# Another order of slots in the first half item, and a group's turns and stores taken in the last item

## The chip, the core and the metric

The kernel runs on one core of a Trainium2 chip. The metric is the device time of one execution in microseconds, as the median of the runs. A core has TensorE (PE in the rows, its weight loads PEld), VectorE (DVE), ScalarE (ACT), GpSimd (POOL) and SyncE (SP), which here issues nearly all DMAs. Each engine works through a program of its own in order and waits on semaphores.

## The reference, cut to what matters

```python
def phi(x):                                # q, k: (4, 4, 1088, 32), r = 8
    a, b = x @ S1.T, x @ S2.T
    return outer(a, b).reshape(..., 64)
num = phi(q) @ (phi(k).T @ v)
den = phi(q) @ phi(k).sum(axis=2) + 1e-6
x = (num / den) -> (4352, 128)             # the heads side by side

P = exp(x @ w_gate - max)                  # (4352, 8 experts)
for _ in range(8):
    P /= P.sum(1) + 1e-9; P /= P.sum(0) + 1e-9; P *= 4352 / 8
out = 0
for e in range(8):
    out += P[:, e:e+1] * (maximum(x @ w1[e], 0) @ w2[e])   # 128 -> 1024 -> 128
```

The weights of expert e are (128, 1024) and (1024, 128), everything is float32. Almost all of the work is the two products of eight experts.

## The kernel before, in words

The attention, the routing and a first part of the experts' work run in the first 189 us. The rest, 189 to 880 us, is the function `weighted`, and the change lies in it alone.

**Groups, items, half items.** The tokens that are left stand in seven groups (`wgroups`), numbered 0 to 6, each with two blocks of n tokens and a list of experts. An item is one expert on one group; there are 40. An item has two half items (s = 0, 1), so t runs from 0 to 79. Group 0 has n = 320, group 4 has n = 320, group 5 has n = 224 and six items (t = 66 to 77), group 6 (`LAST`) has the same tokens as group 5, one expert, and the half items 78 and 79. Its sums are made in another way (`whole`).

**First and second products.** `firsts(t)` makes the products of one half item with the first weights: seven (item 0: eight) products into two PSUM tiles, `pair0` and `pair1`, which ScalarE and VectorE empty. L1171 is the relu on ScalarE, L1174 the sum with relu on VectorE (custom instruction), L1243 to L1252 are copies. They give h0 to h3, and VectorE makes four differences of them, t0 (L1216), t1 (L1219), t2 (L1220) and t3 (L1223). `seconds(t)` multiplies these with the second weights (L1311) and adds the products up in four PSUM tiles, `acc[g][0..3]`, called sums 0 to 3 here.

**Slots.** `seconds(t)` has seven slots. Each slot holds two products of row half 0 and two of row half 1 (rho = 0, 1: partitions 0 to 63 and 64 to 127 of h). The table `order` says which sum m each row half works on in each slot; a 3 stands once for a row half, 0, 1 and 2 twice. Sum 0 needs h0 and h2, sum 1 needs h1 and t0, sum 2 needs t1 and t2, sum 3 needs t3. In TensorE's program the slots of `seconds(t - 1)` alternate with the products of `firsts(t)`, one by one (item 0's second half item starts with two first products, and so does the next).

**The hand-over of a sum.** Both row halves add to the same sum. After the first row half is done with sum m, ScalarE copies one column of it to a tile `turn` (L1363). Nobody uses the value: the other row half's products wait for that copy, and so come after.

**Ring.** h and t live in ten places of the tile `hb`. `turns[t]` lists the seven places of half item t, in the order h0, h2, h3, t0, h1, t2, t3 (t1 replaces h3). A place that an earlier half item has used is free once that one's slots have read it.

**The output of a group.** When a group's four sums are complete, they are copied to SBUF (L1391, L1393), halves of them change places by DMA (`swap_half`, L1412), and `finish_seven` puts nine small sums on the list `leisure`, then for each of the two blocks a sum with the kept part (all L1467) and a turn: `put` turns 32x32 blocks on VectorE (L1495) and issues its stores on SP at once (L738; put off only before item 38). For group 4 the first turn gives eight stores and the second four. An entry of `leisure` whose flag is False, which the turns have, is not taken by GpSimd; it waits at the list's head until VectorE takes it. `aside` gives entries to GpSimd, once or twice in a half item. `spare`, called twice in a half item (after L1216's and after L1223's place), gives VectorE an entry.

**The end.** Group 5's sums are finished in the last item, by begin_next_to_last (L1425) and finish_next_to_last: row sums on VectorE (L1398), `swap_half` in two pairs of DMAs (L1412), the first after sums 0 and 1, the second after 2 and 3, then four sums on GpSimd (L1434), of which the third and fourth need the second pair, one more on VectorE (L1435). `begin_last` adds the results with L1511; behind it on VectorE stand the last sums of group 6 (L1505), the last turns (L1520) and their stores (L738 on SP and ACT).

Of the kernel before, what the change touches and what calls it, by code (L numbers as in the profile page):

```python
# [52 lines left out]
def kernel(  # L53
# [68 lines left out]
    own = consts.tile([P, H], F32, name="own")  # L122
# [36 lines left out]
    for i in range(2):  # L159
        t = wk.tile([P, H + 1, NT + 1, D], F32, name=f"v{i}", bufs=1)  # L160
# [482 lines left out]
    LAST = len(wgroups) - 1  # L643
# [81 lines left out]
    def one_store():  # L725
        if stores:
            stores.pop(0)()
# [348 lines left out]
    def sum_x(i, part_):  # L1076
        xf = sources[i]
        if part_ == 0:
            nc.gpsimd.tensor_tensor(xf[:, 4:6], xf[:, 1:4:2], xf[:, 0:2], op=Alu.subtract)  # L1079
        elif part_ == 1:  # L1080
            nc.vector.tensor_tensor(xf[:, 6], xf[:, 3], xf[:, 4], op=Alu.subtract)
        else:
            nc.vector.tensor_tensor(xf[:, 7], xf[:, 2], xf[:, 6], op=Alu.subtract)
# [27 lines left out]
    def weighted():  # L1111
# [5 lines left out]
        leisure, chores = [(lambda engine, do=do: do(), False) for do in left], []  # L1117
# [8 lines left out]
        for t in range(len(todo)):  # L1126
            if t:
                a0, a1, a2, a3, a4, a5, a6 = turns[-1]
                f0, f1, f2 = unused
                now = [f1, a4, f0, f2, a0, a1, a3] if t == 1 else [f0, f1, f2, a0, a1, a4, a3]  # L1130
                unused = [a2, a5, a6]
            else:
                now, unused = unused[:7], unused[7:]
            turns.append(now)
# [7 lines left out]
        def firsts(t):  # L1142

            i, s = todo[t]
            g, e = witems[i]
            n = wgroups[g][1]
# [29 lines left out]
            def leave(engine, anywhere=False):  # L1176
                if leisure and leisure[0] is None:
                    leisure.pop(0)
                elif leisure and (anywhere or leisure[0][1]):
                    leisure.pop(0)[0](engine)  # L1180
                    return True
# [27 lines left out]
            def spare(spot):  # L1209
                if s == 1 and i + 1 < len(witems):  # L1210
                    sum_x(i + 1, 1 + spot)
                if 0 < g < LAST and (leisure and leisure[0] and not leisure[0][1] if g + 1 == LAST else s == 0):
                    leave(nc.vector, True)

            def first_of_h():
# [66 lines left out]
        def seconds(t):  # L1282

            i, s = todo[t]
            g, e = witems[i]
            lo, n, es = wgroups[g]
# [3 lines left out]
            def fetch(part_):  # L1290
                if coming is not None:
                    load_second(coming, part_)
# [23 lines left out]
            if g in whole and last:  # L1316
                begin_last(g)
                for u, cols in ((0, (0, n)), (1, (0, 128)), (1, (128, n))):
                    m = u + 2 * (cols[0] > 0)
# [24 lines left out]
            def tiles(rho, m, r):  # L1344
                if m == 3:
                    for half in range(2):
                        into(rho, 3, half, raw(1, 1, half), ts[3], half)
                    return
                for half, (f, x) in enumerate((((raw, 0, 0), h[0]), ((raw, 0, 1), h[2]), ((form, 3), h[1]),
                                               ((form, 0), ts[0]), ((form, 2), ts[1]),  # L1350
                                               ((form, 1), ts[2]))[2 * m:2 * m + 2]):
                    into(rho, m, half, f[0](*f[1:], r), x, r)

            order = ((0, 0, 1, 1, 2, 2, 3),) * 2 if narrow(g) else ((0, 0, 2, 2, 1, 1, 3), (1, 1, 3, 0, 0, 2, 2))
            full = [max(k for line in order for k in range(7) if line[k] == m) for m in range(4)]
            for at in range(7):
                for rho in range(2):
                    m = order[rho ^ t % 2][at]
                    tiles(rho, m, order[rho ^ t % 2][:at].count(m))
                yield  # L1360
                if not narrow(g):
                    for m in {1: (0, 1) if t == 0 else (0,), 3: (2,)}.get(at, ()):
                        nc.scalar.copy(turn, acc[g][m][:, 0:1])  # L1363
                for m in range(4):
                    if full[m] == at:
                        fetch(m)
                        if last:
                            ended(g, m)
                for q in range(2 if last else 0):
                    if at == max(full[2 * q:2 * q + 2]) + (narrow(g) and q == 0):  # L1370
                        if narrow(g):
                            add_rows(g, q)
                        swap_half(g, q)
                if last and at == 5 and g + 1 == LAST:
                    begin_next_to_last(g)
                if last and at == 6:
                    (finish_next_to_last if g + 1 == LAST else finish_seven)(g)
                yield
# [3 lines left out]
        def narrow(g):  # L1382
            return 2 * wgroups[g][1] <= 512

        def ended(g, m):
            n = wgroups[g][1]
            if g not in ends:
                ends[g] = late[0].tile([P, 4 * NW], F32, tag="z", name="z", bufs=1)[:, 0:4 * n].rearrange(
                    "p (m n) -> p m n", m=4)
            if not narrow(g):  # L1390
                nc.scalar.copy(ends[g][:, m], acc[g][m][:, 0:n])  # L1391
            elif m % 2:
                nc.scalar.copy(ends[g][:, m - 1:m + 1].rearrange("p m n -> p (m n)"), acc[g][m // 2][:, 0:2 * n])  # L1393

        def add_rows(g, q):
            n = wgroups[g][1]
            z = ends[g][:, 2 * q:2 * q + 2].rearrange("p m n -> p (m n)")
            nc.vector.tensor_tensor(z, acc[g][2 + q][:, 0:2 * n], z, op=Alu.add)  # L1398

        def swap_half(g, q):  # L1400

            n = wgroups[g][1]
            z = ends[g].rearrange("p m n -> p (m n)")[:, 2 * n * q:2 * n * (q + 1)]
            if q == 0:
                swapped.clear()
            if q == 0 or g + 1 < LAST:
                swapped.append(wpool.tile([P, F], F32, tag="w1", name="w1"))
            w = swapped[-1]
            for to, from_, at, lo, hi in ((((lower, upper, n, 0, 2 * n), (upper, lower, 2 * n, 0, n)),
                                           ((lower, upper, 0, 0, n), (upper, lower, 0, 0, 2 * n)))[q] if g + 1 == LAST  # L1410
                                          else ((lower, upper, 0, 0, 2 * n), (upper, lower, 0, 0, 2 * n))):
                nc.sync.dma_start(out=w[to, at:at + hi - lo], in_=z[from_, lo:hi])  # L1412
# [33 lines left out]
        def finish_seven(g):  # L1446
            settle(g)
            n = wgroups[g][1]
            z = ends[g]
            held = []  # L1450

            def own(k, rows=slice(0, P)):
                if not held:
                    held.extend(room(tag, n) for tag in "zxmwf")
                return held[k][rows]

            leisure.extend([None] * 3)
            v = [z[:, m] for m in range(4)]
            x = [w[:, n * a:n * (a + 1)] for w in swapped for a in range(2)]
            lo_, up = lower, upper  # L1460

            def plus_own(k, rows, a, b, op=Alu.add):

                def of(what):
                    return own(what, rows) if isinstance(what, int) else what[rows]

                leisure.append((lambda engine: engine.tensor_tensor(own(k, rows), of(a), of(b), op=op), True))  # L1467

            plus_own(0, lo_, v[0], x[0])
            plus_own(2, lo_, v[0], x[2])  # L1470
            plus_own(2, up, x[0], v[2])
            plus_own(3, lo_, x[1], v[1], Alu.subtract)
            plus_own(2, up, 2, x[2])
            plus_own(1, lo_, 2, 3)
            plus_own(4, up, v[3], x[3])
            plus_own(1, up, 2, v[1])
            plus_own(0, up, 2, 4)
            lo, n, es = wgroups[g]
            for t in range(2):
                at = lo + n * (1 - t)  # L1480
                plus_own(t, slice(0, P), t, kept[0][:, at:at + n])
                leisure.append((lambda engine, t=t, at=at: put(own(t), at, n), False))

        put_at = []

# [4 lines left out]
        def put(y, at, n):  # L1490
            while stores:
                one_store()
            yt = turned_room(len(put_at) % 2, n)
            put_at.append(at)
            nc.vector.transpose(out=yt.rearrange("p b d -> p (b d)"), in_=y)  # L1495
            store(yt, at // 32, (at + n) // 32, put_off=loading[0])
# [28 lines left out]
        for t in range(len(todo)):  # L1525
            i, s = todo[t]
# [161 lines left out]
```

## Time and profile before

| | |
|---|---|
| median of 3 runs | 884.6 us (884.12 to 885.08) |
| the profiled execution | 884.96 us, its span 883.1 us |
| TensorE | 877.0 us busy, 99%, 10828 matmul records |
| VectorE | 722.8 us, 82% |
| ScalarE | 384.7 us, 44% |
| GpSimd | 262.7 us, 30% |
| SyncE | DMA issues only |
| granted TensorE clock | full in all 40 slices |

A row of the timeline has the start in us from the start of the span, the duration, the engine, the line, the operation with the tile written and the tiles read, the shapes, and how many records are merged; in brackets how long the engine was idle before it and who ended that. SPq is SP's issuing of a DMA: its time is that of the issue, not of the transfer. A row of the waits has engine, tile and line, what it waited for, us in total, times, and the longest.

### The profile page before, as it was taken

The page shows a single profiled execution, that of the slowest core. Times are in us where ns is not written, and L with a number is a line of the kernel's source. Part 1 is how long each engine was busy: PE and PEld are TensorE (multiplying, and loading weights), DVE is VectorE, ACT ScalarE, POOL GpSimd, SP SyncE. Part 2 cuts the span into 40 slices and gives each one's busy share as a digit, 9 for nine tenths or more (in the row PEclk, how much of TensorE's full clock was granted, in tenths as well). Part 3 has the DMA queues.
Part 4 walks back from the last instruction along what each step waited for, and adds up shares of the span by engine and source line. Part 5 has one row for each costly group of instructions (what it writes and reads, how often), then busy time and mean ns, then how long its engine had stood idle before and what let it go on. Part 6 is the DMA issues. An engine that isn't in the chain of part 4 may idle for free.

```text
span 883.1 us, 26157 instructions
## 1 busy us (share of the span) xinstructions
PE 877.0 (99%) x10828; PEld 582.2 (66%) x10828; DVE 722.8 (82%) x981; ACT 384.7 (44%) x791; POOL 262.7 (30%) x255
## 2 busy tenths in 40 slices
PE   9999999999999999999999999999999999999998
PEld 6778656867788655555555555555555566668996
DVE  8699689978888887788877778888788888888896
ACT  3455457644444533333343333334443354444442
POOL 3131115454533213222222222221323323311431
PEclk9999999999999999999999999999999999999999
DMA  8889299886666654444435544434755557557762
GB/s 250 279 264 279 76 231 255 132 250 199 195 193 196 173 166 130 132 147 123 127 98 144 137 125 125 119 115 108 194 152 148 149 143 216 152 155 217 216 187 57
DMA packets 120887, 149.08 MB, mean 169 GB/s; under 512 B 52288, under 2 KB 79808, under 8 KB 120384
## 3 DMA queue, kind: packets, MB, share of 16 engines
q1 hardware_dynamic: 112656, 136.92, 54.4%
q0 software_dynamic: 6720, 10.19, 5.8%
q8 instruction: 86, 1.41, 0.7%
q10 hardware_dynamic: 1392, 0.28, 0.2%
q14 instruction: 33, 0.27, 0.1%
HBM read 104.86 MB, written 25.99 MB: 148 GB/s over the span
## 4 chain that ended last, share of the span: by engine, by line
PE 97%; DMA 1%; DVE 1%; SPq 0%; issue 0%; DVEq 0%
PE pair L1158 39%; PE s L1311 38%; PE a L772 9%; PE s L836 7%; PE a L336 1%; PE a L465 1%; DMA v<-in_v_dram 1%; DMA qx<-in_q_dram 0%; DMA w1x<-w1x 0%; PE a L429 0%; PE a L306 0%; PE s L395 0%; PE s L1323 0%; PE s L375 0%; PE a L499 0%
## 5 line engine op out<-in xcount | busy, mean ns | idle before, releaser
L1158 PE MATMUL pair<-xf,w1x 64*64 64x320 f32 (+3 forms) x4496 | 580.2, 466 | 0.5 <-DVE hb L1174 0.4
L1311 PE MATMUL s<-hb,w 64*64 64x480 f32 (+3 forms) x2544 | 366.1, 466 | 0.0
L1158 PEld LDWEIGHTS pair<-xf,w1x 64*64 64x64 f32 x4496 | 258.6, 133 | 113.3 <-issue 63.5
L1174 DVE CUSTOM_DVE_ANT_0 hb<-pair,copies 128x960 f32<-128x960 f32 (+3 forms) x234 | 214.7, 918 | 103.0 <-PE pair L1158 90.3
L1311 PE MATMUL s<-hb,ws 64*64 64x480 f32 (+3 forms) x1888 | 282.5, 468 | 0.0
L1311 PEld LDWEIGHTS s<-hb,w 64*64 64x64 f32 x2544 | 155.3, 133 | 73.2 <-issue 38.6
L1311 PEld LDWEIGHTS s<-hb,ws 64*64 64x64 f32 x1888 | 116.1, 133 | 55.3 <-issue 29.3
L1071 POOL TENSOR_TENSOR xf<-xT,pb 128x960 f32<-128x960 f32 (+3 forms) x40 | 70.2, 1756 | 241.3 <-ACT turn L1363 184.4
L1079 POOL TENSOR_TENSOR xf<-xf 128x960 f32<-128x960 f32 (+3 forms) x39 | 68.4, 1755 | 224.1 <-ACT turn L1363 155.4
L1171 ACT ACTIVATE hb<-pair 128x640 f32<-128x640 f32 (+3 forms) x86 | 66.4, 773 | 151.4 <-PE pair L1158 149.5
L772 PE MATMUL a<-xT,w 128*64 128x416 f32 (+3 forms) x512 | 122.9, 465 | 0.0
L774 ACT ACTIVATE hb<-a 128x416 f32<-128x416 f32 (+3 forms) x128 | 59.5, 468 | 65.8 <-PE a L772 60.6
L1216 DVE TENSOR_TENSOR hb<-hb 128x960 f32<-128x960 f32 (+3 forms) x78 | 76.5, 981 | 7.9 <-PE pair L1158 0.9
L1363 ACT COPY turn<-s 128x1 f32<-128x1 f32 x133 | 20.7, 156 | 137.3 <-PE s L1311 137.2
L1223 DVE TENSOR_TENSOR hb<-hb 128x960 f32<-128x960 f32 (+3 forms) x78 | 72.4, 928 | 7.4
L1219 DVE TENSOR_TENSOR hb<-hb 128x960 f32<-128x960 f32 (+3 forms) x78 | 74.8, 959 | 2.9 <-ACT hb L1171 1.2
L1252 ACT COPY copies<-pair 128x960 f32<-128x960 f32 (+3 forms) x78 | 59.9, 768 | 35.8 <-PE pair L1158 35.6
L1248 ACT COPY copies<-pair 128x960 f32<-128x960 f32 (+3 forms) x78 | 60.1, 770 | 33.0 <-PE pair L1158 33.0
L1243 ACT COPY copies<-pair 128x960 f32<-128x960 f32 (+3 forms) x78 | 59.9, 768 | 33.0 <-PE pair L1158 28.8
L836 PE MATMUL s<-hb,ws 128*64 128x416 f32 (+3 forms) x224 | 71.6, 474 | 0.0
L1220 DVE TENSOR_TENSOR hb<-hb 128x960 f32<-128x960 f32 (+3 forms) x78 | 71.4, 915 | 0.0
L787 DVE TENSOR_TENSOR hb<-hb 128x416 f32<-128x416 f32 (+7 forms) x84 | 56.9, 680 | 13.1 <-ACT hb L774 10.4
(205 smaller groups left out, 662.2 us busy)
## 6 DMA issues: line engine op xcount, KB each, us to landing
w1x<-w1x SPq DMA_DIRECT2D x87, 256.0 KB, 3.6
w<-w2x SPq DMA_DIRECT2D x71, 256.0 KB, 3.0
ws<-w2x SPq DMA_DIRECT2D x35, 256.0 KB, 3.4
pb<-pT SPq DMA_DIRECT2D x14, 480.0 KB, 3.8
xf<-xf SPq DMA_DIRECT2D x28, 240.0 KB, 3.3
w1x<-w1x SPq DMA_DIRECT2D x7, 896.0 KB, 6.0
ws<-w2x SPq DMA_DIRECT2D x36, 128.0 KB, 3.8
pb<-pT SPq DMA_DIRECT2D x13, 320.0 KB, 4.0
```

The lines of the kernel that those rows point to most:

```text
L772: nc.tensor.matmul(ph[sl], loaded_w[j][0][:, P * f + H2 * s:P * f + H2 * (s + 1)], xT[:, at + lo:at + hi], start=True, stop=True, tile_pos ...
L836: nc.tensor.matmul(sums[g][i][H2 * s:H2 * (s + 1)], w, x, start=c == 1, stop=c == per, tile_position=(0, H2 * s))
L1071: nc.gpsimd.tensor_tensor(xf[:, 0:2].rearrange("p b n -> p (b n)"), xT[:, lo:lo + 2 * n], weights.pop(i), op=Alu.mult)
L1079: nc.gpsimd.tensor_tensor(xf[:, 4:6], xf[:, 1:4:2], xf[:, 0:2], op=Alu.subtract)
L1158: nc.tensor.matmul(out[H2 * col:H2 * (col + 1), r], w1[rows, PLACE[form], o:o + H2], xf[rows, x], start=start, stop=stop, tile_position=(H ...
L1171: nc.scalar.activation(out=x, in_=y, func=Act.Relu)
L1174: nc.vector._custom_dve(TENSOR_ADD_SAT, out=flat(out, n), in0=x, in1=flat(y, n), s0=math.inf, s1=0.0)
L1216: nc.vector.tensor_tensor(ts[0], h[3], h[0], op=Alu.subtract)
L1219: nc.vector.tensor_tensor(ts[1], h[3], h[1], op=Alu.subtract)
L1220: nc.vector.tensor_tensor(ts[2], h[1], ts[0], op=Alu.subtract)
L1223: nc.vector.tensor_tensor(ts[3], h[2], ts[2], op=Alu.subtract)
L1311: nc.tensor.matmul(out_[H2 * half:H2 * (half + 1)], w[rows], flat(x, n)[rows, r], start=c == 1, stop=True, tile_position=(H2 * rho, H2 * h ...
```

## The change

Three things change.

1. In half item 0 (t = 0) the table `order` is another. Row half 0 goes through the sums as 0, 0, 1, 1, 3, 2, 2 (it was 0, 0, 2, 2, 1, 1, 3) and row half 1 as 1, 1, 2, 2, 0, 0, 3 (it was 1, 1, 3, 0, 0, 2, 2). A hand-over copy for sum 3 is added after slot 4.
2. Half item 1 takes other places of the ring: its h2 that of half item 0's h0 (it was h1's), its h1 that of h1 (it was h0's), its t2 that of t0 (it was h2's) and its t3 that of h2 (it was t0's).
3. For group 4 the two turns go to the end of `leisure`, behind both sums, and `spare` no longer gives VectorE anything in group 5; in group 6 it does so in the first half item (t = 78). In the built order the turns leave VectorE's program in half items 75 and 76 and stand in half item 78, one ahead of the first L1398, one behind it. SP's eight stores of the first turn come ahead of the first pair of L1412, and the four of the second between the two pairs; three loads of second weights (L974, L971, L977), which stood behind or between them, come ahead. The order of GpSimd's instructions stays.

```diff
-                now = [f1, a4, f0, f2, a0, a1, a3] if t == 1 else [f0, f1, f2, a0, a1, a4, a3]
+                now = [f1, a0, f0, f2, a4, a3, a1] if t == 1 else [f0, f1, f2, a0, a1, a4, a3]
...
-                if 0 < g < LAST and (leisure and leisure[0] and not leisure[0][1] if g + 1 == LAST else s == 0):
+                if s == 0 and 0 < g != LAST - 1:
                     leave(nc.vector, True)
...
-            order = ((0, 0, 1, 1, 2, 2, 3),) * 2 if narrow(g) else ((0, 0, 2, 2, 1, 1, 3), (1, 1, 3, 0, 0, 2, 2))
+            order = ((0, 0, 1, 1, 2, 2, 3),) * 2 if narrow(g) else (
+                ((0, 0, 1, 1, 3, 2, 2), (1, 1, 2, 2, 0, 0, 3)) if t == 0 else ((0, 0, 2, 2, 1, 1, 3), (1, 1, 3, 0, 0, 2, 2)))
...
-                    for m in {1: (0, 1) if t == 0 else (0,), 3: (2,)}.get(at, ()):
+                    for m in ({1: (0, 1), 3: (2,), 4: (3,)} if t == 0 else {1: (0,), 3: (2,)}).get(at, ()):
                         nc.scalar.copy(turn, acc[g][m][:, 0:1])
...
+            puts = []
             for t in range(2):
                 at = lo + n * (1 - t)
                 plus_own(t, slice(0, P), t, kept[0][:, at:at + n])
-                leisure.append((lambda engine, t=t, at=at: put(own(t), at, n), False))
+                (puts if g + 2 == LAST else leisure).append((lambda engine, t=t, at=at: put(own(t), at, n), False))
+            leisure.extend(puts)
```

## The prediction

> **What bounds the kernel now.** I read the page first, then the waits of all engines, then the timeline of TensorE around the first half item and over the last four, and last the timelines of SP, POOL and VectorE behind it.
>
> ```profile
> span 883.1 us, 26157 instructions
> PE 877.0 (99%) x10828; PEld 582.2 (66%) x10828; DVE 722.8 (82%) x981; ACT 384.7 (44%) x791; POOL 262.7 (30%) x255
> PE 97%; DMA 1%; DVE 1%; SPq 0%; issue 0%; DVEq 0%
> PEld s L1311 <- DVE hb L1223: 1.4, 5, 0.5
> PE pair L1158 <- DVE hb L1174: 0.4, 1, 0.4
> ```
>
> TensorE is busy for 877.0 of 883.1 us, and 97% of the chain that ended last is its own work. So the time is the sum of three things: TensorE's fixed work, the few stalls in it, and what lies behind its last matmul. The last two rows name two stalls, and the change touches one place each: the order of slots of half item 0 (the wait on L1223) and the turns of group 4's output (the wait on L1174). What lies behind the last matmul must be looked at too, since the second edit moves DMAs there. 0.2% of 884.6 is 1.8 us; that is about what a measurement of this kernel can tell from no change.
>
> **Part one, the order of slots.** A slot is four products (eight matmul records); second products of half item t-1 alternate with first products of half item t.
>
> ```profile
> 194.63 0.79 PE L1311 MATMUL s<-hb,w 64*64 64x320 f32 x8
> 196.79 1.15 PE L1311 MATMUL s<-hb,ws 64*64 64x320 f32 x6
> 203.43 0.75 PE L1311 MATMUL s<-hb,w 64*64 64x320 f32 x8
> 203.97 0.75 PE L1158 MATMUL pair<-xf,w1x 64*64 64x320 f32 x8
> 196.52 0.41 PEld L1311 LDWEIGHTS s<-hb,ws 64*64 64x64 f32 x4
> 197.45 0.14 PEld L1311 LDWEIGHTS s<-hb,ws 64*64 64x64 f32 x2 [0.52 <-DVE hb L1223]
> 196.23 1.16 DVE L1223 TENSOR_TENSOR hb<-hb 128x640 f32<-128x640 f32 x1
> 196.46 0.35 ACT L1363 COPY turn<-s 128x1 f32<-128x1 f32 x2 [0.61 <-PE s L1311]
> ```
>
> From 194.63 to 196.79 are four slots, 2.16, so a slot is 0.54; 203.43 to 203.97 gives the same. Slot 2 of half item 0 starts at 196.79 and half item 1's slot 0 at 203.43; eleven slots lie between (five second, six first), which is 11 x 0.538 = 5.92, and it took 6.64. The loss of 0.72 is in slot 2: row half 1 is at sum 3 there, which needs the difference t3 of L1223, done at 196.23 + 1.16 = 197.39, and the weights are loaded at 197.45, 0.06 later. In the new order sum 3 stands in slots 4 and 6, at 196.79 + 2 x 1.08 = 198.94 at the earliest, when t3 has been there for 1.5 us. That wait goes.
>
> What is late next: slot 2 now holds sum 1 for row half 0, and row half 1 wrote that sum in slots 0 and 1. The ACT copy that hands sum 1 over is the second of the two at 196.46, done at 196.81, and the built order shows that wait on the first matmul of slot 2. Everything behind it on TensorE's queue waits too. The load now goes at 196.52 and would go at 196.81 + 0.06 = 196.87. That bounds the new stall by 0.35; but a load is 0.27 ahead of its matmul here, and one that comes late is used about 0.05 after it starts, so matmul 196.79 becomes 196.92: I take 0.13. Gain 0.72 - 0.13 = 0.59, bounds 0.37 and 0.72. The one added ACT copy, half of those 0.35, is for sum 3 after slot 4; its taker is slot 6, two slots of each kind later (1.08), and the relu that it follows needs only the product before slot 4: nothing. The exchanged ring places make half item 1's h1 wait for slot 3 in place of slot 4, its t2 too, and leave h2 and t3 at slot 5; each is as early or earlier. Nothing. From there to 856 TensorE has no stall, and its suppliers wait for it, so they move along.
>
> **Part two, what leaves group 5.** The two turns (L1495) go from half items 75 and 76.
>
> ```profile
> 856.15 0.61 PE L1311 MATMUL s<-hb,w 64*64 64x224 f32 x8
> 857.15 0.61 PE L1158 MATMUL pair<-xf,w1x 64*64 64x224 f32 x8 [0.39 <-DVE hb L1174]
> 857.58 0.56 PE L1311 MATMUL s<-hb,ws 64*64 64x224 f32 x8
> 854.06 0.50 DVE L1495 STREAM_TRANSPOSE r<-z 128x320 f32<-128x320 f32 x1
> 854.49 0.58 DVE L1219 TENSOR_TENSOR hb<-hb 128x448 f32<-128x448 f32 x1
> 856.48 1.15 DVE L1174 CUSTOM_DVE_ANT_0 hb<-pair,copies 128x448 f32<-128x448 f32 x2
> 857.96 0.56 PE L1158 MATMUL pair<-xf,w1x 64*64 64x224 f32 x8
> ```
>
> A slot here is 857.96 - 857.58 = 0.38. From 856.15 to 857.58 are two, 0.76, and took 1.43: 0.67 lost. TensorE waits for the first relu-add (L1174), which starts at 856.48 because VectorE comes through late, with no idle time. The turn holds VectorE from 854.06 to 854.49: 0.43. Without it the chain comes 0.43 earlier and 0.24 of the stall stays. Gain 0.43, bounds 0.3 and 0.67. The second turn, at 859.02, made no stall. Both parts: 0.59 + 0.43 = 1.02, bounds 0.7 and 1.4.
>
> **Part three, what arrives in the last item.** Each turn brings its stores, issued by SP in program order: eight DMAs for the first, four for the second. In the built order SP now has: the eight stores, the first pair of L1412 (halves that change places for group 5's sums), the four stores, the second pair of L1412, the final stores. Before, all twelve stood well ahead of L1412.
>
> ```profile
> 869.26 0.61 DVE L1398 TENSOR_TENSOR z<-s,z 128x448 f32<-128x448 f32 x1
> 854.58 3.70 SPq L738 DMA_DIRECT2D out_dram<-r  x8
> 860.94 1.85 SPq L738 DMA_DIRECT2D out_dram<-yt  x4
> 869.90 0.47 SPq L1412 DMA_DIRECT2D w<-z  x1
> 870.42 1.62 SPq L1412 DMA_DIRECT2D w<-z  x1
> 872.13 1.19 SPq L1412 DMA_DIRECT2D w<-z  x2
> 858.39 1.63 SPq L974 DMA_DIRECT2D w<-w2x  x1
> q8 instruction: 1, 0.02, 4.3%
> q8 instruction: 1, 0.02, 4.4%
> q8 instruction: 1, 0.02, 5.4%
> 875.13 0.66 POOL L1434 TENSOR_TENSOR m<-m,w 128x224 f32<-128x224 f32 x1
> 875.86 0.66 POOL L1434 TENSOR_TENSOR w<-w,m 64x224 f32<-64x224 f32 x1
> 876.56 0.39 DVE L1511 TENSOR_TENSOR kept<-kept,w 128x224 f32<-128x224 f32 x1 [0.23 <-POOL w L1434]
> 876.87 0.38 DVE L1511 TENSOR_TENSOR kept<-kept,m 128x224 f32<-128x224 f32 x1
> 877.55 0.39 DVE L1505 TENSOR_TENSOR kept<-s,kept 128x224 f32<-128x224 f32 x1 [0.29 <-PE s L1323]
> 877.97 0.41 DVE L1520 STREAM_TRANSPOSE r<-kept 128x224 f32<-128x224 f32 x1
> 879.37 0.28 DVE L1520 STREAM_TRANSPOSE yt<-kept 128x96 f32<-128x96 f32 x1
> ```
>
> How to read it: the second pair of L1412 (872.13) feeds POOL's third L1434 (875.13), POOL's fourth feeds L1511, and every last sum, turn and store (L1505, L1520) stands behind L1511 on VectorE. In before L1511 is done at 877.25 and L1505 waits 0.29 more for TensorE: that is all the slack there is.
>
> I walk SP's queue on the old clock (positions relative to TensorE's work). The first turn takes the place of L1398 at 869.26 and ends 0.50 later, 869.76. Eight stores: 3.70, to about 873.5. First pair: 0.47 and about 0.6, with gaps of 0.05 to 0.1, to 874.7. Four stores: 1.85, to 876.6. Second pair: from about 876.7 for 1.19, to 877.9. In before POOL's third sum starts 875.13 - 873.32 = 1.81 after that pair's issue; so 879.7. POOL to the end of L1434: 876.52 - 875.13 = 1.39, so 881.1. Two L1511: 877.25 - 876.53 = 0.72, so L1505 starts at 881.8 in place of 877.55. From there to the last turn VectorE works without a gap worth naming (877.55 to 879.65 in six steps that follow each other), so the end is 4.3 later.
>
> Two SP issues of 1.62 and 1.63 stand beside ones of 0.4 to 0.6. The rows of queue q8 are, in order, those of the DMA view for 858.3 to 860.1, 870.3 to 872.1 and 876 to 877.1: in each lies one instruction packet. I read these as an issue that is held while instructions are fetched, 1.1 to 1.2 us more. With SP issuing without a break from 869.8 to 878, the packet after 870.3 meets a store, and the one after 876 a store or a pair. None, one or two of them: 0, 1.2 or 2.3; I take one. The Trainium skill ("Runtime: NRT & Kernel Launch", section "Instruction fetch mechanics") says that crossing a block of instructions costs one bump of a DMA's tail and is mostly hidden. By that rule the term would be 0 and the sum 4.3; the two rows of 1.6 us speak against it, without proving the cause.
>
> The turns cost VectorE 0.43 each in half item 78 as well, and the sums between are held, so the first relu-add of half item 79 comes some 0.35 late and TensorE can stall up to 0.3. Its cover is the queue's delay: TensorE's last sums wait on VectorE for over 4 us anyway. Without the queue's delay it would cost those 0.3.
>
> **The sum.** The profiled run is 884.96 us with a span of 883.1, so 1.86 lies around it; it is 0.36 above the median of the runs, 884.6. Span: 883.1 - 1.02 + 4.3 + 1.2 = 887.6. Time for such a run 889.4, against the median **889.1 us**, 0.5% slower.
>
> **Rivals.** *The queue delays, nothing is fetched meanwhile:* 884.6 - 1.02 + 4.3 = 887.9. For it: most issues in the trace have 0.4 to 0.6; against: two of the seven SP rows above. *Both fetches hit, and the second pair lands behind the four stores:* 884.6 - 1.02 + 4.3 + 2.3 = 890.2, and some tenths for the landing. *Not slower:* the stores cost the tail no time, since SP passes them within the 2.3 us between the first turn (869.8) and the second pair's old place (872.13); then only the two stalls go: 884.6 - 1.02 + 0.3 (the stall in half item 79) = 883.9, no change that can be told. It decides when twelve issues take under 2.3 + 0.3 us of slack, 0.2 each. The rows have 0.46 each, so I give it little. *Faster by over 0.2%:* beside that the rest of the stall at 857.15 and the new wait on the ACT copy would have to go, 0.24 and 0.13: 884.6 - 1.4 = 883.2 is still inside 0.2%, so only something that I don't see gives it. *The first part does nothing* (the ACT copy holds as long as L1223 did): 0.59 more on the forecast, 889.7.
>
> **Chances.** Queue with one fetch 0.40 (the first part without effect, 0.05, in it), with none 0.25, with both 0.25, not slower 0.08, faster 0.02. So slower 0.90, same 0.08, faster 0.02. The range takes in the three queue cases: low, none with the larger gain, 884.6 - 1.4 + 4.1 = 887.3, less 0.3 for a landing that is quicker; high 890.2 with a gain of 0.7 and 0.3 for the landing, 890.8. I give 887.0 to 890.8.
>
> **What the changed profile would show.** The weight load's wait on L1223 gone, and 11 slots after the third group in about 6.05 in place of 6.64; the stall before half item 76's last products near 0.25; TensorE's last matmul about a microsecond earlier, unless half item 79 stalls. In SP's rows eight stores ahead of the first L1412 and four between the pairs, the second pair issued at 876 to 879; POOL's third L1434 idle on that DMA; L1505 after L1511 no longer waiting for TensorE; and DMA, SP and POOL in the chain that ended last. It is wrong if the second pair is issued before 874, or if L1505 still waits for TensorE.

## The result, and the profile after

The changed kernel takes 889.46 us, the median of 6 runs (888.76 to 890.86); the kernel before takes 884.68 us beside it (884.12 to 886.34). The ratio is 1.0054, with a 95% interval of 1.0041 to 1.0067: slower by 4.8 us. The forecast was 889.1, range 887.0 to 890.8.

Line numbers of after are those of before plus 1 from L1355 on and plus 3 from L1483 on, so L1412 is L1413 here, L1511 is L1514 and L1505 is L1508. The profiled execution took 890.86 us. Its first lines on the page:

```profile
span 889.1 us, 26157 instructions
PE 875.9 (99%) x10828; PEld 583.9 (66%) x10828; DVE 723.0 (81%) x981; ACT 384.6 (43%) x792; POOL 262.6 (30%) x255
```

TensorE is busy for 1.1 us less than before (877.0), and the span is 6.0 longer. Of that, 0.7 lies ahead of everything the change touches: slot 0 of half item 0 starts at 195.31 here and at 194.63 before. The same start lay between 193.4 and 195.3 in the ten traces of this study, so all positions below are counted from it.

**The start.** The timeline of TensorE, its weight loads and ScalarE around half item 0:

```profile
195.31 0.79 PE L1311 MATMUL s<-hb,w 64*64 64x320 f32 x8
203.63 0.75 PE L1311 MATMUL s<-hb,w 64*64 64x320 f32 x8
197.54 0.20 PEld L1311 LDWEIGHTS s<-hb,w 64*64 64x64 f32 x4 [0.39 <-ACT turn L1364]
197.14 0.35 ACT L1364 COPY turn<-s 128x1 f32<-128x1 f32 x2 [0.61 <-PE s L1311]
```

From slot 0 of half item 0 to that of half item 1 are 15 slots, 15 x 0.538 = 8.07; they take 8.32, so 0.25 is lost. Before it was 203.43 - 194.63 = 8.80, so 0.73. The wait on L1223 is gone, and the load of slot 2 now waits for the ScalarE copy: that ends at 197.49, the load goes at 197.54. Between these two traces the difference is 0.48; e_turns below shows that not every execution of the old order loses 0.73.

**Half item 76.** TensorE's timeline where before lost 0.67:

```profile
856.33 0.61 PE L1311 MATMUL s<-hb,w 64*64 64x224 f32 x8
856.94 0.61 PE L1158 MATMUL pair<-xf,w1x 64*64 64x224 f32 x8
857.37 0.56 PE L1311 MATMUL s<-hb,ws 64*64 64x224 f32 x8
```

Two slots of 0.38 take 857.37 - 856.33 = 1.04: 0.28 is lost. Gain 0.39.

**The tail.** SP's timeline (issues, not transfers), then the rows of queue q8 in the DMA view for 870.8 to 872.4 and for 875.4 to 876.9, then VectorE and GpSimd:

```profile
869.28 5.14 SPq L738 DMA_DIRECT2D out_dram<-r  x8
874.52 1.10 SPq L1413 DMA_DIRECT2D w<-z  x2
875.71 3.07 SPq L738 DMA_DIRECT2D out_dram<-yt  x4
878.88 1.11 SPq L1413 DMA_DIRECT2D w<-z  x2
q8 instruction: 1, 0.02, 5.8%
q8 instruction: 1, 0.02, 6.0%
868.75 0.50 DVE L1498 STREAM_TRANSPOSE r<-z 128x320 f32<-128x320 f32 x1
881.80 0.66 POOL L1435 TENSOR_TENSOR m<-m,w 128x224 f32<-128x224 f32 x1 [2.02 <-DMA w<-z]
883.22 0.39 DVE L1514 TENSOR_TENSOR kept<-kept,w 128x224 f32<-128x224 f32 x1 [7.32 <-POOL w L1435]
883.83 0.38 DVE L1508 TENSOR_TENSOR kept<-s,kept 128x224 f32<-128x224 f32 x1
885.36 0.28 DVE L1523 STREAM_TRANSPOSE yt<-kept 128x96 f32<-128x96 f32 x1
```

SP issues without a break from 869.28 to 879.99: eight stores, a pair, four stores, a pair. The second pair is done 6.67 us later than before (873.32), or 5.99 counted from slot 0. GpSimd waits for it, VectorE stands idle for 7.32 us behind GpSimd, and L1508 no longer waits for TensorE, whose sums have been there for microseconds. The chain that ended last has the same piece of the queue at its end:

```profile
878.88 0.47 SPq L1413
879.39 2.25 DMA w<-z
881.80 0.66 POOL m L1435
```

### The profile page after: what moved, and what is told of

Read it like the earlier page. It is cut to its first block, busy times and chain, and to the rows that moved or that the text cites. A ratio compares the mean times of both kernels' runs of the same rounds, so it can differ in the third digit from the quotient of the medians.

```text
span 889.1 us, 26157 instructions
## 1 busy us (share of the span) xinstructions
PE 875.9 (99%) x10828; PEld 583.9 (66%) x10828; DVE 723.0 (81%) x981; ACT 384.6 (43%) x792; POOL 262.6 (30%) x255
## 4 chain that ended last, share of the span: by engine, by line
PE 96%; DMA 2%; DVE 0%; SPq 0%; issue 0%; POOLq 0%; POOL 0%; DVEq 0%; ACT 0%; ACTq 0%
PE pair L1158 39%; PE s L1311 38%; PE a L772 9%; PE s L836 7%; DMA qx<-in_q_dram 1%; PE a L465 1%; PE a L336 1%; DMA v<-in_v_dram 0%; PE a L429 0%; PE a L306 0%; PE s L395 0%; SPq L738 0%; DMA raw<-in_S_dram 0%; DMA w<-z 0%; PE a L499 0%; DVE kT L289 0%
## 5 line engine op out<-in xcount | busy, mean ns | idle before, releaser
L1311 PE MATMUL s<-hb,w 64*64 64x480 f32 (+3 forms) x2544 | 366.3, 466 | 0.0
L1311 PE MATMUL s<-hb,ws 64*64 64x480 f32 (+3 forms) x1888 | 282.3, 468 | 0.0
L1311 PEld LDWEIGHTS s<-hb,w 64*64 64x64 f32 x2544 | 155.3, 133 | 73.3 <-issue 42.8
L1311 PEld LDWEIGHTS s<-hb,ws 64*64 64x64 f32 x1888 | 116.2, 133 | 54.2 <-issue 32.4
L1223 DVE TENSOR_TENSOR hb<-hb 128x960 f32<-128x960 f32 (+3 forms) x78 | 72.4, 928 | 7.4
L1220 DVE TENSOR_TENSOR hb<-hb 128x960 f32<-128x960 f32 (+3 forms) x78 | 71.9, 922 | 0.0
```

What stands on the lines that cost most here:

```text
L1220: nc.vector.tensor_tensor(ts[2], h[1], ts[0], op=Alu.subtract)
L1223: nc.vector.tensor_tensor(ts[3], h[2], ts[2], op=Alu.subtract)
L1311: nc.tensor.matmul(out_[H2 * half:H2 * (half + 1)], w[rows], flat(x, n)[rows, r], start=c == 1, stop=True, tile_position=(H2 * rho, H2 * h ...
```

## Experiments

The theory: the slowdown is made in SP's program order alone. Stores that stand ahead of the second pair of halves put off its issue; everything behind is a fixed chain. The rivals: the two turns hold VectorE or GpSimd, the stores' transfers slow the exchange of halves, or the new order of slots costs time of its own.

**e_order: the first two parts alone.**

The edit, against the changed kernel:

```diff
-                if s == 0 and 0 < g != LAST - 1:
+                if 0 < g < LAST and (leisure and leisure[0] and not leisure[0][1] if g + 1 == LAST else s == 0):
...
-            puts = []
...
-                (puts if g + 2 == LAST else leisure).append((lambda engine, t=t, at=at: put(own(t), at, n), False))
+                leisure.append((lambda engine, t=t, at=at: put(own(t), at, n), False))
-            leisure.extend(puts)
```

> Part one alone on the kernel before: the new order of slots, the ring places and the added turn copies; the turns of group 4's output stay in half items 75 and 76. Theory (SP's queue in the last item makes the whole slowdown): only the loss in slot 2 of half item 0 changes, from 0.72 to the 0.24 seen in the trace of after, so 0.5 us less than before: 884.2 us, a ratio of 0.9995, which cannot be told from no change by the time. The 11 slots behind slot 2 take about 6.1 us in place of 6.64, and L1505 still waits for TensorE at the end. Rival (the new order costs time of its own later, by its ACT copies or its ring places): above 885.5, and part of the 4.8 us is here.

Measured: 883.92 us against 884.53, ratio 0.9995 (0.9986 to 1.0003), on the forecast and not to be told from no change. Rows of TensorE's and VectorE's timeline of e_order:

```profile
194.56 0.79 PE L1311 MATMUL s<-hb,w 64*64 64x320 f32 x8
202.87 0.75 PE L1311 MATMUL s<-hb,w 64*64 64x320 f32 x8
877.24 0.39 DVE L1506 TENSOR_TENSOR kept<-s,kept 128x224 f32<-128x224 f32 x1
```

The 15 slots take 8.31, as in after. But the gain doesn't all last: counted from slot 0, TensorE falls 0.25 behind after's places between half items 2 and 8, and its last L1311 comes at 680.62, where before has 680.85. e_turns falls behind by 0.28 over the same half items, the other traces by at most 0.05; why stays open. The wait for TensorE ahead of the last sums, which I expected to stay, is not there (L1506 has no bracket). The rival's time, above 885.5, is not reached.

**e_turns: the third part alone.**

The edit, against the changed kernel:

```diff
-                now = [f1, a0, f0, f2, a4, a3, a1] if t == 1 else [f0, f1, f2, a0, a1, a4, a3]
+                now = [f1, a4, f0, f2, a0, a1, a3] if t == 1 else [f0, f1, f2, a0, a1, a4, a3]
...
-            order = ((0, 0, 1, 1, 2, 2, 3),) * 2 if narrow(g) else (
-                ((0, 0, 1, 1, 3, 2, 2), (1, 1, 2, 2, 0, 0, 3)) if t == 0 else ((0, 0, 2, 2, 1, 1, 3), (1, 1, 3, 0, 0, 2, 2)))
+            order = ((0, 0, 1, 1, 2, 2, 3),) * 2 if narrow(g) else ((0, 0, 2, 2, 1, 1, 3), (1, 1, 3, 0, 0, 2, 2))
...
-                    for m in ({1: (0, 1), 3: (2,), 4: (3,)} if t == 0 else {1: (0,), 3: (2,)}).get(at, ()):
+                    for m in {1: (0, 1) if t == 0 else (0,), 3: (2,)}.get(at, ()):
```

> The moved turns alone on the kernel before: order of slots, ring places and turn copies stay as they were, both turns and their twelve stores come in half item 78. Theory (parts are independent, the whole loss is the queue's): after plus the 0.48 us of slot 2, about 890.0 us, 889.5 to 890.5, a ratio of 1.006; the loss of 0.72 in slot 2 and the wait on L1223 are back. Rival (the new order adds to the slowdown): below 889.

Measured: 889.64 us against 884.34, ratio 1.0054 (1.0042 to 1.0067), inside the range. The whole slowdown is in this part. Rows of TensorE's, VectorE's and SP's timeline of e_turns:

```profile
194.08 0.79 PE L1311 MATMUL s<-hb,w 64*64 64x320 f32 x8
202.45 0.75 PE L1311 MATMUL s<-hb,w 64*64 64x320 f32 x8
195.59 0.82 DVE L1223 TENSOR_TENSOR hb<-hb 128x640 f32<-128x640 f32 x1
868.39 4.86 SPq L738 DMA_DIRECT2D out_dram<-r  x8
874.55 2.95 SPq L738 DMA_DIRECT2D out_dram<-yt  x4
```

At the start the trace is not what I expected: the order of slots is the old one, and yet the loss of 0.72 is not back, and the waits of that stretch list none on L1223. The 15 slots take 8.37, so 0.30 is lost, none of it in slot 2. L1223 took 0.82 here and t3 was done 2.33 after slot 0; in before it took 1.16 and was done 2.76 after. The 0.43 between them is the 0.43 by which the two traces differ. So the stall that part one removes hangs on when VectorE is done with t3 in that execution. In the eight traces with the new order t3 is done 2.67 to 3.30 after slot 0 and nothing waits for it in slot 2; by the same step the old order would have lost some 0.3 to 1.0 there. That is an estimate, since none of them ran the old order.

TensorE's last L1311 comes 0.35 later than in after, counted from slot 0, and yet the last turn starts at the same place (884.07 - 194.08 = 689.99; after 885.36 - 195.31 = 690.05). SP's two rows say why: the twelve stores took 7.81 here and 8.21 in after, so 0.40 less, and that cancels the 0.35.

**e_nostore: the twelve stores left out.** The edit, against the changed kernel, as in those that follow:

```diff
-            store(yt, at // 32, (at + n) // 32, put_off=loading[0])
+            if loading[0]:
+                store(yt, at // 32, (at + n) // 32, put_off=True)
```

> The changed kernel with the twelve stores of group 4's output left out (that part of the output is not written); the two turns on VectorE stay in half item 78. Theory (the stores stand ahead of the second pair of halves on SP): the second pair is issued near 872, L1508 waits for TensorE again, and the time is 884.7 - 0.5 - 0.4 = 883.8 us, up to 0.3 more for a stall in half item 79. Rival (the turns hold VectorE, or POOL's sums are late for a reason of their own): 888 to 889.5, with the second pair early and L1508 still late.

Measured: 882.96 us against 884.53, ratio 0.9982 (0.9974 to 0.9991). Rows of SP's and VectorE's timeline of e_nostore:

```profile
867.88 3.29 SPq L1413 DMA_DIRECT2D w<-z  x4
875.18 0.39 DVE L1515 TENSOR_TENSOR kept<-kept,w 128x224 f32<-128x224 f32 x1 [1.19 <-POOL w L1435]
877.32 0.28 DVE L1524 STREAM_TRANSPOSE yt<-kept 128x96 f32<-128x96 f32 x1
```

The two turns are still in half item 78, and the idle time of VectorE ahead of the last sums falls from 7.32 to 1.19. The last turn starts 683.90 after slot 0, in before 684.74. So the turns by themselves cost the end nothing that shows. The last sums (L1509 here) do not wait for TensorE, though I had expected it; they follow L1515, which waits for GpSimd. I had 883.8; the time is 0.8 lower. Slot 0 started at 193.42 in this trace, 1.2 earlier than before, so the trace can't say whether that 0.8 belongs to the edit.

**e_defer: the same stores behind the second pair.** Order on SP: four halves, twelve stores, last stores.

```diff
-            while stores:
+            while loading[0] and stores:
                 one_store()
...
-            store(yt, at // 32, (at + n) // 32, put_off=loading[0])
+            store(yt, at // 32, (at + n) // 32, put_off=True)
...
-                while stores:
+                while stores and t + 1 < len(todo):
                     one_store()
...
         def finish_next_to_last(g):
+            while stores:
+                one_store()
...
-                ends[g, u] = turned_room(u, n)
+                ends[g, u] = room("wf"[u], n).rearrange("p (b d) -> p b d", d=32)
```

> The changed kernel with the same twelve stores in the same stretch, but issued by SP behind the second pair of halves instead of ahead of it and between the pairs; the last output goes through two other buffers, so that it need not wait for the stores. Theory (the order on SP's queue): second pair near 872.3, then twelve stores of 5.55 us, and up to two holds of 1.15: SP is free between 878 and 880.2, and the last stores are issued from about 879. So 883.8 to 885 us. Rival (the stores' transfers, not their place in the queue, slow the exchange of halves): 887 to 889, with the second pair issued early and POOL's third sum still more than 3 us behind it.

Measured: 885.08 us against 884.53, ratio 1.0006 (0.9997 to 1.0015), 0.1 above the theory's range and far from the rival's 887 to 889. Rows of SP's and VectorE's timeline of e_defer:

```profile
868.85 3.71 SPq L1413 DMA_DIRECT2D w<-z  x4
872.59 4.86 SPq L738 DMA_DIRECT2D out_dram<-r  x8
877.50 1.98 SPq L738 DMA_DIRECT2D out_dram<-yt  x4
880.58 0.89 SPq L738 DMA_DIRECT2D out_dram<-f  x2
878.05 0.28 DVE L1525 STREAM_TRANSPOSE f<-kept 128x96 f32<-128x96 f32 x1
```

The same bytes move, from 872.59 on beside the second pair's, and GpSimd's third sum still starts 1.92 after that pair's issue (874.47 - 872.55), where before has 1.81. The last turn is no later than it was (878.05 - 194.35 = 683.70; before 879.37 - 194.63 = 684.74). So it is the place in the queue, not the transfers. But SP is at the twelve stores until 879.48, and the last output, turned by 878.33, is issued at 880.58: the delay has moved behind the turn, 2.2 us of it.

**e_dose: only the second turn (four stores) late.**

```diff
-                if s == 0 and 0 < g != LAST - 1:
+                if s == 0 and 0 < g and (g != LAST - 1 or i + 2 == len(witems) and leisure and leisure[0] and not leisure[0][1] and spot == 0):
```

> The changed kernel with the first turn (eight stores) taken in half item 76 and only the second (four stores) in half item 78, at its first place, so that four stores stand ahead of both pairs of halves on SP. Theory (the queue, with the moment at which the halves are ready): the four stores run from about 869.0 to 870.9, 872 with a fetch; the pairs then need 3.1 us to 874 or 875.2, where they are done by 872.2 when nothing stands ahead; 0.3 to 0.8 of that is slack, so 883.4 + 0.8 to 2.0 = 884.2 to 885.4. A third of the stores costs less than a third of the 6 us. Rival (each turn moved late costs its share): 883.4 + 2 to 3 = 885.5 to 886.5.

Measured: 884.20 us against 884.34, ratio 1.0003 (0.9994 to 1.0012): the lower end of the theory's range, well below the rival's. Rows of SP's and VectorE's timeline of e_dose:

```profile
867.74 0.59 DVE L1399 TENSOR_TENSOR z<-s,z 128x448 f32<-128x448 f32 x1
867.84 1.82 SPq L738 DMA_DIRECT2D out_dram<-yt  x4
869.77 3.21 SPq L1413 DMA_DIRECT2D w<-z  x4
876.21 0.39 DVE L1514 TENSOR_TENSOR kept<-kept,w 128x224 f32<-128x224 f32 x1 [1.82 <-POOL w L1435]
878.34 0.28 DVE L1523 STREAM_TRANSPOSE yt<-kept 128x96 f32<-128x96 f32 x1
```

A third of the stores costs less than a sixth of the loss: 884.2 stands 0.8 above e_best's 883.4 below (the kernel before ran 0.2 faster beside this one), where after stands 6.0 above it. The first halves are ready at 867.74 + 0.59 = 868.33, and the pairs start at 869.77: 1.4 late. 0.69 of that is slack in before, as the next run shows, and 0.75 is left. Seven of the eleven runs took 883.8 to 884.4, the profiled one among them, and four took 885.5 to 886.3; what those four met is not known.

**e_double: each of the twelve stores issued twice.**

```diff
             store(yt, at // 32, (at + n) // 32, put_off=loading[0])
+            if not loading[0]:
+                store(yt, at // 32, (at + n) // 32)
```

> The changed kernel with each of the twelve stores issued twice, the same bytes to the same place: sixteen, the first pair, eight, the second pair. Theory (SP's issues one after another set when the second pair goes): twelve more issues at 0.46 is 5.5 us more, 889.5 + 5.5 = 895.0, and 0 to 1.2 for one more fetch: 895 to 896.2. Rival (transfers or turns, not issues): a transfer of this size adds under 1 us where the turns stay two, so below 891.

Measured: 895.85 us against 884.34, ratio 1.0123 (1.0110 to 1.0137), inside the theory's range. Rows of SP's and VectorE's timeline of e_double:

```profile
868.07 9.59 SPq L738 DMA_DIRECT2D out_dram<-r  x16
877.76 1.11 SPq L1413 DMA_DIRECT2D w<-z  x2
878.96 4.05 SPq L738 DMA_DIRECT2D out_dram<-yt  x8
883.07 1.11 SPq L1413 DMA_DIRECT2D w<-z  x2
889.54 0.28 DVE L1525 STREAM_TRANSPOSE yt<-kept 128x96 f32<-128x96 f32 x1
```

The chain behind the second pair is of fixed length wherever the queue is what is late. From the end of the second pair's issue to the start of the last turn it takes 885.36 - 879.99 = 5.37 in after, 5.36 here (889.54 - 884.18) and 5.36 in e_dose (878.34 - 872.98). In before it is 879.37 - 873.32 = 6.05: the 0.69 more is the slack that TensorE's last sums leave.

**e_noring: the new order without the new ring places.**

The edit, against e_order:

```diff
-                now = [f1, a0, f0, f2, a4, a3, a1] if t == 1 else [f0, f1, f2, a0, a1, a4, a3]
+                now = [f1, a4, f0, f2, a0, a1, a3] if t == 1 else [f0, f1, f2, a0, a1, a4, a3]
```

> Part one without the exchanged ring places, on the kernel before: the new order of slots and the turn copies only. Half item 1's h1 then takes the place of a tile that half item 0 reads until slot 5 in place of slot 3. Theory (the exchange belongs to the new order): a wait in half item 1 on those products, and TensorE loses up to 1.1 us more (two slots of each kind) between its first and its second half item. Rival (the places are free early enough anyway): 15 slots from half item 0's slot 0 to half item 1's take 8.3 us as with the exchange, and no new wait appears.

Measured: one time, 886.75 us. In this kernel half item 1's h1 and t2 are written, in program order, to the places of half item 0's h0 and h2 ahead of the slots that read those for sum 0, so the sum 0 of half item 0 is made of other values. Rows of TensorE's and its weight loads' timeline of e_noring:

```profile
193.65 0.79 PE L1311 MATMUL s<-hb,w 64*64 64x320 f32 x8
205.14 0.75 PE L1311 MATMUL s<-hb,w 64*64 64x320 f32 x8
202.41 0.13 PEld L1311 LDWEIGHTS s<-hb,w 64*64 64x64 f32 x1 [2.56 <-DVE hb L1220]
```

The 15 slots take 11.49, 3.2 more than with the exchange, against the 1.1 I allowed. I had the mechanism wrong too: it isn't half item 1 that waits for a place to come free, but half item 0's products that wait for half item 1's t2 (L1220). The exchange of ring places is a part of the new order, not a refinement of it.

**e_best: part one, and both turns in half item 76.**

```diff
-                if s == 0 and 0 < g != LAST - 1:
+                if s == 0 and 0 < g and (g != LAST - 1 or i + 2 == len(witems) and leisure and leisure[0] and not leisure[0][1]):
...
-                    for m in ({1: (0, 1), 3: (2,), 4: (3,)} if t == 0 else {1: (0,), 3: (2,)}).get(at, ()):
+                    for m in ({1: (1, 0), 3: (2,), 4: (3,)} if t == 0 else {1: (0,), 3: (2,)}).get(at, ()):
```

> The changed kernel with both turns of group 4's output taken in half item 76 (item 38, where no partial sums of the next input are formed) in place of half item 78, and with the two turn copies of half item 0 in the other order, sum 1 first. The twelve stores then stand well ahead of the exchange of halves. Theory: the tail is that of before, the loss in slot 2 is 0.24 or 0.1 in place of 0.72, the stall before half item 76's last products keeps 0.28 in place of 0.67, and the two turns may stall half item 77 by up to 0.4: 884.7 - 0.5 - 0.4 = 883.7 us, bounds 883.4 and 884.2; the best of the kernels. Rival (a late turn costs time on VectorE wherever it stands behind half item 75): 885 or more.

Measured: 883.43 us against 884.53, ratio 0.9993 (0.9984 to 1.0002). Rows of e_best's timeline: TensorE, a weight load, SP and the last turn.

```profile
194.80 0.79 PE L1311 MATMUL s<-hb,w 64*64 64x320 f32 x8
203.00 0.75 PE L1311 MATMUL s<-hb,w 64*64 64x320 f32 x8
196.91 0.20 PEld L1311 LDWEIGHTS s<-hb,w 64*64 64x64 f32 x4 [0.27 <-ACT turn L1364]
858.77 3.71 SPq L738 DMA_DIRECT2D out_dram<-r  x8
862.90 2.64 SPq L738 DMA_DIRECT2D out_dram<-yt  x4
869.11 3.13 SPq L1413 DMA_DIRECT2D w<-z  x4
878.59 0.28 DVE L1523 STREAM_TRANSPOSE yt<-kept 128x96 f32<-128x96 f32 x1
```

The twelve stores are through by 865.5, ahead of the first halves at 869.1. With sum 1 copied first the load waits 0.27 in place of 0.39, and the 15 slots take 8.20. The last turn starts 683.79 after slot 0, in before 684.74: against that trace of before 0.95 is gone, and no tail has come for it. It is 6 us faster than the changed kernel (5.4 by the two ratios); against the kernel before it gains 0.07% by the ratio and 0.1% by the trace, and the interval still holds no change.

## Why the prediction was right

**The bound and the mechanism.** The step that mattered, the stores ahead of the second pair of L1412 in SP's order, is what happened, and e_nostore, e_defer and e_double show it from three sides: without the stores, with the stores elsewhere in the queue, with twice as many.

**Part one.** Predicted gain 0.59 (bounds 0.37 and 0.72); the two traces differ by 0.48. The new wait is as I had it: the copy ends 2.18 after slot 0, the load follows 0.05 later, the first matmul of slot 2 comes at 197.55 in place of 195.31 + 4 x 0.538 = 197.46, and the first products behind it at 198.14 in place of 198.00, which is the 0.13 that I took. (I had let a late load be used 0.05 after it starts; here it is 0.01.) What I had wrong is that the 0.72 lies in slot 2 and is there in every run. 0.43 of it is L1223's, and e_turns, with the same order, hasn't got that part. The other 0.3 is lost ahead of half item 1, where a load of first weights waits 0.35 (at 202.84 in before, at 201.86 in e_turns); after keeps 0.11 of it. So over the two traces of the old order this part gave 0.48 and 0.05, and the times can't tell it from nothing. For the slowdown of 4.8 it matters little.

**Part two.** Predicted gain 0.43 with 0.24 left; measured 0.39 with 0.28 left. The 0.39 is lost in the three kernels that have the first turn in half item 75 (before, e_order, e_noring) and in none of the seven others. I didn't predict two things beside it. A loss of 0.30 in half item 78, which before has, is gone in after and in every other kernel here with a turn in that half item (e_turns, e_nostore, e_defer, e_dose, e_double), and there in the three without (e_order, e_noring, e_best). The relu-add that TensorE waits for there waits for the same products in before, after and e_best, and why it starts later in two of them stays open. The stall that I feared for half item 79 (up to 0.3) is 0.08. So TensorE's last L1311 comes 1.11 earlier, where 1.02 was forecast.

**Part three.** By its steps, on the clock of slot 0: the span grew by 6.0 - 0.7 = 5.3, and TensorE came 1.1 earlier, so the tail is 6.4 longer; the forecast had 4.3 + 1.2 = 5.5. The term that was mis-sized is the one for held issues. The eight stores took 5.14 where 3.70 is their time undisturbed, the four 3.07 where it is 1.85: 1.44 + 1.22 = 2.7 us more, where I took 1.2 for one hold. 2.5 of that is two held issues, 1.70 in place of 0.42 at 871.07 and 1.56 in place of 0.33 at 875.71; the rest is a pause ahead of the seventh store. Both q8 packets fell on a store. They did so in the traces of e_turns (1.43 and 1.35) and e_double too. That was the rival "both fetches hit", 890.2, and the profiled run of 890.86 (with its late start of 0.7) is that case. The other five runs of after took 888.8 to 890.1; how much was held in them is not known.

Two smaller things went the other way by about 0.5 together: the queue ran a little tighter than my walk, and the last sums, no longer waiting for TensorE, took 883.83 to 885.64 = 1.81 where before they took 2.10. The delay from the second pair's issue to GpSimd's third sum is 881.80 - 879.99 = 1.81, the same as in before. So the median came within 0.4 of the sum partly by luck: a hold was missing from the sum, and against it stood a tail walked 0.5 too long and 0.30 that went in half item 78 unforeseen. The low end of the range took 4.1 for the tail where the walk gives 4.3; with 4.3 it is 887.2, and nothing hangs on it.

The Trainium skill ("Runtime: NRT & Kernel Launch", section "Instruction fetch mechanics") calls the cost of a new block of instructions mostly hidden. By that rule the tail would be 2.5 shorter. Here SP's queue is the path, and the two held issues, each beside an instruction packet, speak against the rule for such a place; that the fetch makes them is not shown.

## What to carry to other kernels

A turn or a copy that is moved takes its DMA issues along, and those are queued in program order on the engine that issues them: cost the issues (0.46 us each here, twelve of them 5.5 us), and ask what stands behind them on that queue, above all in the last microseconds, where nothing runs ahead to cover it. The cost starts only where the thing behind is ready: four stores ahead of the same pairs cost about 0.8 us, twelve cost 6. And a table of buffer places goes with the order of use that it was made for: change one and the other has to follow.

## What the runs showed that I hadn't expected

**Held issues.** Counted over the ten traces, from 190 us on: of 241 SP issues that started between 0.1 us before and 0.4 us after the start of an instruction packet on q8, 140 took over 0.9 us, and these ended 0.38 us (median) after the packet did. Of 4257 issues that started neither in such a packet nor in the 0.3 us before one, 61 took over 0.9, and the median is 0.42. Of 219 that started 0.5 us or more into a packet, 29 took over 0.9. So the hold (0.9 to 1.3 us in the issues named above) goes with the packet; that fetching instructions causes it wasn't tried, since no kernel here moved a fetch alone.

**A queue with no cover is exact.** In three kernels the second pair's issue ends 679, 685 and 690 us after slot 0, and the chain behind it is the same to 0.01 us (5.36, 5.37, 5.36).
